# Three groups of narrow matmuls per batch instead of eight, in a kernel whose order is written out by hand

## The chip, the cores and the metric

The kernel runs on one core of one Trainium2 chip. The metric is the device time of one execution in microseconds (us), the median of several runs. PE is the matmul engine (PEld its weight loads), DVE the vector engine, ACT the activation engine, POOL the general-purpose engine, SP the engine whose queue issues all the DMAs here. PSUM is the memory that PE writes to; it has eight banks of 512 fp32 columns, and DVE and ACT empty it.

## The reference

Attention between 512 tokens and 32 state vectors in both directions, and then a two-layer network with a softplus between the layers, over all 8 x (512 + 32) rows.

```
# x: (8, 8, 512, 64), state: (8, 8, 32, 64); w_in: (512, 2048), w_out: (2048, 512)
scores = scale * np.matmul(x, state.transpose(0, 1, 3, 2))
a = softmax(scores)                      # over the 32 states
xread = np.matmul(a, state)
scores2 = scale * np.matmul(state, x.transpose(0, 1, 3, 2))
a2 = softmax(scores2)                    # over the 512 tokens
sread = np.matmul(a2, x)
rows = concatenate([xread, sread], axis=2)   # heads side by side: 512 columns
h = rows @ w_in
out = (log(1 + exp(h)) @ w_out).astype(np.float32)
```

## The kernel before

One batch has 512 token rows (and 32 state rows). The token rows never form `xread`: the kernel multiplies the state by `w_in` first (*state product*, `v_product`, letter v; it gives two PSUM banks for 512 of the 2048 columns), splits the result into a high and a low part (`v_hi` h, `v_lo` l), and multiplies those by the softmax weights (*gemm1*, letter g: six matmuls of 128x512 for 128 of the 2048 columns, into one PSUM bank). Softplus (s, ACT) reads that bank.

For batches 0 and 1 the second layer is *gemm2* (G) with `w_out` split in high and low parts. Batches 2 to 7, and the state rows of all batches (called batch 8), go another way: per batch seven sums of blocks (*forms*, F), each split (H high, L low) and multiplied by a combination of `w_out` blocks that lies in HBM as a *slab* (J loads it, 1 MB). A *product* (M) is half a form: eight pairs of matmuls, one of 512 columns with the high part and one of 256 with the low part. Fourteen products make a batch. `chain` (k) adds the results from PSUM, `fold` (q) adds halves, `fold_store` (P) stores.

The attention of one batch is four kinds of *narrow* PE work. *Scores* (Q, eight matmuls with tiles of 64 rows by 32 columns, two PSUM banks; they need the x loads T). The same tiles make the state product v, four units of eight matmuls per batch. Two *transposes* (t) of the column softmax; the *read* (R, 32 matmuls with 128x32 tiles); one transpose of the read's result (`s_back`, y). The softmax over states goes `a_turn` (1), `a_max` (2), `a_sub` (3), `a_exp` (4), `a_sum` (5), `a_mul` (6), `a_back` (7), `a_hi` (8), `a_lo` (9); the one over tokens `s_max` (e), `s_exp` (f), `s_sum` (i). The exponentials (4 and f) and softplus need different tables on ACT. In the profile an fp32 matmul leaves two records, so a v or a scores step shows as x16; gemm1 and the products show as what they are. gemm1 reads `b<-d,d`, gemm2 `b<-g,s`, products `b<-g,d`, v `b<-W,ST`, scores `b<-d,ST`, transposes `b<-ident`, the read `b<-d,s`.

Nothing schedules this kernel: the string `PLAN` has a letter for each step, and the last loop runs the steps in that order; every engine executes its share strictly in that order (class `Ordered`). Which of two engines does a step is looked up in `ENG` by the letter and its count (A is ACT, D is DVE, P is POOL; for the raw weights g and d name the pool). Buffers come from four pools with fixed numbers of rooms (`N1`, `N2`, `N4`, `N8`) and from the eight banks, first freed first taken, in the order of the plan. Every recorded operation has line 99, that of the class that records the order, so groups are told by their tiles.

```
    for k in PLAN:
        now[0] = k
        count[k] = count.get(k, 0) + 1
        next(run[k])
```

Of the kernel before, what the change touches and what calls it, by code (L numbers as in the profile page):

```python
# [37 lines left out]
PLAN = (
    "TSTISTTIIQII1IQ2Ie3OaXbfI1Ic4tO2vuOQ5hhOIla6IbI73aSc88O4e9vOa9Ohh5fatlla6ub7ac88b1919cgblcavbbgIehhlflcAgcAsbt"
    "XBcgIBICumvCDnDEsEhGmhslsGnmBAIenGOlBfgiCAmigDsCEGDsnaEgbO2OG2a3casGb3bOgacbGBcAcmRsCvnDGBAmTEhmGrAlhnGml4nAg4"  # L40
    "CnDgBTsEjBGCsCDBGjDmEAEgn5aGjsCt65GDujaGEbO6bOgaabOcAGjcsbGccjmBGOmBCAOnvDnjvAEhmChGhlhDAjlGllgEBjnAGsCBTgDCmE"
    "jgDBTnsEvsCQXihDXihGlmjleEGjefG1n17gXmf7XAjBGn88CsG9j9BGiAmignjDCtsEGDuEjG223g34jGgs5jt6sGu4QojvopNeGNphhefgjl"
    "olopUgpfm1yjtsWRzKYRZvKrs1njmuvhNGhmlhlhjGllnmgNjrUGsnGmWnKgYGNKsNnGmUgnWNvsNKYGhhlKGmlUmgnWGnsNKYGNKg5GUms6nG"
    "WmKgYnKGsNGNUmgnWGsKYGmKnNgGsGN7Ug8m79WGnsKG8YmJ9gKNNGsnJmUyGzZWngJYKGsKmGnJgitisGuGgGsGgGsyGz2Z32g34GsG5o6voH"
    "pogph7hplovlsp4LghghlslgFs5gsH6gs7LgsgFsgsHFgsLgsgsMsHFLMJFFHFMXLHJkXkSHMHJLHLFMJHkkqLPMHJqLPRJHkkvLMHrLhhllMJ"
    "HLMJkkLLyMJ8z89Z9MJkkqkPkqMPJvJkkMqhqhPlPlMTTJgJkkqvqsPgPhhlglsgsgsHvsLghhlglsgsgsHgsLgsgFsgsHgsLgsgFsFMsHFLQJ"
    "FMeHefLMXFJkXkF1f1HMHJHLHLMJHkkqLPMHJqLPiitFJtuMkuHkLLMJHLLRJHkkMr223L4yMJz3Z455vJk6Mhkhkqk6PllqMJ7P78899vJkkM"
    "qhqhPlPlMTTJgJkkqvqsPgPhlhglsgsgsHvsLghhlglsgsgsHgsLgsgFsgsHgsLgsgFsFMsHFLQJFMeHefLMXFJkXkF1f1HMHJHLHFLMJHMHkJ"
    "kqLPtqJktuPMkHuLLMJHiiLLRHJkMkrL22y3MJzL4Z354vJMk6hkhkqkqPlPMlJ5768vJkkMqh7hqPl8Pl9MT9TJgJkkqvqsPgPhlhglsgsgsH"
    "vsLghhlglsgsgsHgsLgsgFsgsHgsLgsgFsFMsHFLQJFMeHefLMXFJkXkF1f1HMHJHLHFLMJHMHkJkqLPtqJktuPMkHuLLMJHiiLLRHJkMkrL22"  # L50
    "y3MJzL4Z354vJMk6hkhkqkqPlPMlJ5768vJkkMqh7hqPl8Pl9MT9TJgJkkqvqsPgPhlhglsgsgsHvsLghhlglsgsgsHgsLgsgFsgsHgsLgsgFs"
    "FMsHFLQJFMeHefLMXFJkXkF1f1HMHJHFLHwMJHkxkMHJLLqtqJtwkPMukHPuLwLMJHxiiLLRHJwkMxrkL2xyMJ2zZ334L4vJkMkhqkhPkqlPwl"
    "Mx55v6Mh6hkkqlPlqM7P78899vkwgkqhxhPlqwgslwPxgxsgsJgswxvsghhlJglsgsgsJgsgsgsJgsgsgsgsgsgswwxxgswwxxgswwxxgswHHx"
    "LLgsHHLLgFFsHHLgFLsMFsHHLLFFMJFFFFHMJkkHkLLFFHMJFLHHLHHFLHMJHHkHHkFkLMJqFqPqPHLHMHPLJHkkkLLMJLHHLLLMHJHkkkLLLM"
    "JLLLMJkkqkPkqkkqMPPMkkqkPqqMPPMkqMPkqkqPP"
)
ENG = {
    '3': "PPPPPDPDPDPDPDDD",
    '6': "DDPPDPPDPPPPPPDD",
    '8': "AAAAAAAAAAAAAAAAAA",  # L60
    '9': "PPPPDDPDDDDDDDDDDD",
    'D': "AAPDDAAAAPPDAPAD",
    'E': "DDDDDDDDDDDDDPDD",
    'F': "DDDDDDPDDDDDDDPDDDDDDDPPDDDDDDPPDDDDDDPPPDPDDDDDDDDDPPPP",
    'H': "DAAAAAAAAAAAAAAAAAAADAAAAPAAAAAAAADAAAAPAAAAAAAADAAAAPAAAAAAAADAAAAPAADADDAAADAPAAAAAAAAPAAAPAAAAP",
    'I': "ggggggggggdgdddg",
    'L': "DDDDDDDDDDDDDDDDDDDDDDDDDDDDDDDDDDDDDDDDDDDDDDDDDDDDDDDDDDDDDDDDDDDDDDDDDDDDDDDDDDDDDDDDDDDDDDDDDD",
    'N': "DPDDDDDDDDDDDDDD",
    'O': "gggggddgggddddgg",
    'U': "DDDDDDDD",  # L70
    'W': "DDAAAAAA",
    'Y': "DDDDDDDD",
    'h': "AAAAAAADDAAAAAAAAAAAAAAAAADAAAAAADAAAAAADAAAAAAADAAAAAAADAAAAAAAAAAD",
    'k': "AADDDDDDDDDDDDDDAADDDDDDDDDDDDDDAADDDDDDDDDDDDDDAADDDDDDDDDDDDDDAADDDDDDDDDDDDDDADADDDDDDDDDDDDDDDDDDDDD",
    'm': "AAAAAPPADAAPAPPDPAPAAAAAAAAAAAAA",
    'n': "DDPDDDDDDDDDDPDDPDDDDDDDDDDDDDDD",
    'o': "DAAADAAA",
    'q': "PDPPPDPDPDPPPDPDPDPPPPPDPDPPPPPDDDPPPPPPDDDPPPPDDDDD",
    'u': "AAAADADAAAAAAAAA",
    'w': "AAAPAAAPPDDDDDDD",  # L80
    'x': "PPPPPDDDDDDDDDDD",
    'z': "DAAAAAAA",
}


# [898 lines left out]
```

## Time and profile before

| | |
|---|---|
| runs | 635.24 us median of 3 (634.68 to 636.11) |
| profiled execution | 634.05 us, its span 632.3 us |
| busy in the span | PE 613.6 us, DVE 486.6, ACT 326.8, POOL 123.0 |
| chain that ended last | PE 83% of the span, DVE 1%, ACT 1% |
| ACT_TABLE_LOAD | 36, of 1.28 us each |

The page's busy time of PE counts matmuls whose ends are modelled, and neighbours overlap in it. Prices of PE work are therefore read from starts: from the start of one line of the timeline to the start of the next. From about 200 us on the batches repeat with a period of some 69.5 us.

### The profile page before, as it was taken

What the parts mean: (1) busy time and instruction counts of PE and PEld (TensorE: products, weight loads), DVE (VectorE), ACT (ScalarE), POOL (GpSimd) and SP (SyncE); (2) the same over time, 40 slices, a digit from 0 to 9 for tenths busy, and PEclk for the clock granted to TensorE, in tenths of its full rate; (3) what the DMA queues carried; (4) which work ended last, traced back from release to release, by engine and by line L of the source; (5) the groups of instructions that cost most, each with busy time, mean ns of one, the idle gap of its engine ahead of it and who ended that gap; (6) DMA issues with size and microseconds to landing.
All of it is one profiled execution on the core that took longest, in us unless ns stands there. A gap on an engine that the chain in (4) does not pass through costs nothing.

```text
span 632.3 us, 10553 instructions
## 1 busy us (share of the span) xinstructions
PE 613.6 (97%) x4072; PEld 485.3 (77%) x4072; DVE 486.6 (77%) x741; ACT 326.8 (52%) x497; POOL 123.0 (19%) x108
## 2 busy tenths in 40 slices
PE   3799999999999999999999999999999999999997
PEld 1477777778878887888777877788778877998886
DVE  5999898999366964499638994599549994289993
ACT  4799969454375613662357434562367335332700
POOL 1121222100000200011202230042203522014440
PEclk9999999999999999999999999999999999999999
DMA  8999472645910998079923996099905947005672
GB/s 314 407 407 348 155 242 71 217 144 181 346 68 12 412 403 338 2 288 420 329 95 131 396 381 224 7 355 403 360 8 210 404 169 281 2 3 167 215 314 69
DMA packets 48049, 146.96 MB, mean 232 GB/s; under 512 B 4224, under 2 KB 28288, under 8 KB 37248
## 3 DMA queue, kind: packets, MB, share of 16 engines
q1 hardware_dynamic: 48000, 146.29, 61.8%
q8 instruction: 32, 0.52, 0.3%
q14 instruction: 17, 0.14, 0.1%
HBM read 122.68 MB, written 23.59 MB: 231 GB/s over the span
## 4 chain that ended last, share of the span: by engine, by line
PE 83%; DVE 1%; ACT 1%; issue 0%
PE b L99 83%; DVE s L99 1%; DVE d L99 1%; ACT L99 0%; ACT s L99 0%; DVE g L99 0%; ACT d L99 0%
## 5 line engine op out<-in xcount | busy, mean ns | idle before, releaser
L99 PE MATMUL b<-g,d 128*128 128x512 f32 x1344 | 252.1, 340 | 0.1
L99 PEld LDWEIGHTS b<-g,d 128*128 128x128 f32 x1344 | 205.7, 188 | 41.7 <-issue 10.9
L99 PE MATMUL b<-d,d 128*128 128x512 f32 x768 | 185.9, 394 | 1.9 <-ACT d L99 1.8
L99 PEld LDWEIGHTS b<-d,d 128*128 128x128 f32 x768 | 143.6, 189 | 43.3 <-issue 5.8
L99 DVE TENSOR_TENSOR d<-g,d 128x1024 fp32r<-128x1024 f32 x72 | 99.0, 1388 | 44.9 <-ACT d L99 44.5
L99 PE MATMUL b<-g,s 128*128 128x512 f32 x496 | 123.7, 382 | 0.8 <-DVE g L99 0.7
L99 PEld LDWEIGHTS b<-g,s 128*128 128x128 f32 x496 | 87.9, 188 | 25.4 <-issue 4.2
L99 ACT ACTIVATE g<-b 128x512 f32<-128x512 f32 x96 | 57.0, 597 | 77.9 <-PE b L99 77.8
L99 ACT CAST d<-g 128x1024 fp32r<-128x1024 f32 x59 | 61.2, 1050 | 33.7 <-PE b L99 16.3
L99 DVE TENSOR_TENSOR s<-s,b 128x512 f32<-128x512 f32 x91 | 57.4, 677 | 27.2 <-PE b L99 27.2
L99 POOL TENSOR_TENSOR g<-g,g 128x1024 f32<-128x1024 f32 x10 | 25.9, 2592 | 141.6 <-DVE g L99 81.8
L99 ACT CAST d<-b 128x512 fp32r<-128x512 f32 (+2 forms) x60 | 30.7, 561 | 33.4 <-PE b L99 33.3
L99 ACT ACT_TABLE_LOAD x35 | 44.9, 1283 | 2.3 <-DVE v L99 1.7
L99 POOL TENSOR_TENSOR s<-s,v 128x512 f32<-128x512 f32 x19 | 20.6, 1089 | 128.2 <-DVE v L99 111.4
L99 DVE TENSOR_TENSOR d<-b,d 128x512 fp32r<-128x512 f32 (+2 forms) x68 | 41.6, 650 | 3.5 <-ACT d L99 2.5
L99 POOL TENSOR_TENSOR s<-s 128x256 f32<-128x256 f32 x32 | 23.8, 752 | 101.2 <-DVE s L99 89.0
L99 PE MATMUL b<-W,ST 64*32 64x512 f32 (+2 forms) x544 | 36.3, 590 | 2.7 <-DVE W L99 2.7
L99 DVE TENSOR_TENSOR d<-d,d 128x1024 fp32r<-128x1024 f32 (+1 forms) x22 | 27.1, 1243 | 1.0 <-ACT d L99 0.9
L99 ACT ACTIVATE s<-b 128x512 f32<-128x512 f32 x32 | 18.6, 599 | 14.2 <-PE b L99 14.0
L99 ACT COPY s<-b 128x512 f32<-128x512 f32 x32 | 17.8, 589 | 14.8 <-PE b L99 14.6
L99 ACT CAST d<-d 128x1024 fp32r<-128x1024 f32 x18 | 18.8, 1048 | 10.6 <-DVE d L99 8.0
L99 DVE TENSOR_TENSOR s<-s,s 128x512 fp32r<-128x512 f32 x31 | 21.8, 709 | 2.4 <-ACT s L99 2.4
(77 smaller groups left out, 521.4 us busy)
## 6 DMA issues: line engine op xcount, KB each, us to landing
g<-slabs SPq DMA_DIRECT2D x84, 1024.0 KB, 8.9
d<-in_xt_dram SPq DMA_DIRECT2D x16, 512.0 KB, 6.2
d<-in_xn_dram SPq DMA_DIRECT2D x16, 512.0 KB, 7.2
slabs<-d SPq DMA_DIRECT2D x16, 512.0 KB, 3.2
g<-in_w_in_dram SPq DMA_DIRECT2D x12, 512.0 KB, 10.4
slabs<-g SPq DMA_DIRECT2D x24, 256.0 KB, 5.5
out_dram<-s SPq DMA_DIRECT2D x48, 128.0 KB, 4.3
g<-in_w_out_dram SPq DMA_DIRECT2D x10, 512.0 KB, 10.2
```

What stands on the lines that cost most here:

```text
L99: return lambda *a, **k: self.tc.keep_in_program_order(f(*a, **k))
```

## The change

Only the plan, the table of engines and two pool sizes change. From batch 2 on the narrow work of a batch stands in three groups: scores and two state products; the back transpose of the batch before and the two transposes; the read and two state products. Before it stood in eight: scores; two transposes; the read; the back transpose; four state products one by one. The order of all other steps is laid out anew around this, in the first 200 us and the last batch too, and many steps change between ACT, DVE and POOL. `N2` goes from 18 rooms to 20, `N4` from 14 to 13. No function is touched, and the matmuls are the same ones.

```
-N1, N2, N4, N8 = 4, 18, 14, 8
+N1, N2, N4, N8 = 4, 20, 13, 8
 PLAN = (
...
-    "vsLghhlglsgsgsHgsLgsgFsgsHgsLgsgFsFMsHFLQJFMeHefLMXFJkXkF1f1HMHJHLHFLMJHMHkJkqLPtqJktuPMkHuLLMJHiiLLRHJkMkrL22"
-    "y3MJzL4Z354vJMk6hkhkqkqPlPMlJ5768vJkkMqh7hqPl8Pl9MT9TJgJkkqvqsPgPhlhglsgsgsHvsLghhlglsgsgsHgsLgsgFsgsHgsLgsgFs"
...
+    "kkJqqPPMJgJkkqgqsPPgsQsvevefghhlhghlflgls1g1siHsgsiLgs2H23gs34gLgFs5gs6sg47HgLs5gsFMss6FHMXLJFFMXkJFkHFHMFLJHH"
+    "HytJztLuMukkqLPMJZqLPLMHJkkLH7RHJLvrvhhMHLllMJhhkllkMJHLMJ8k8kqkPkq9MPLTJ9MTkkJqqPPMJgJkkqgqsPPgsQsvevefghhlhg"
...
 )
 ENG = {
-    'h': "AAAAAAADDAAAAAAAAAAAAAAAAADAAAAAADAAAAAADAAAAAAADAAAAAAADAAAAAAAAAAD",
+    'h': "AAAAAAADAAAAAADADAADAAADAAAADAADDAAADADDDAAADADDDAAADADDDAAAAAAADAA",
...
```

Of the plan two lines of each side are shown; with the line that follows they hold one batch of the middle.

On PE, at the scores of a batch in the middle (the tiles that ST stands beside are the x of that batch for scores and `w_in` for the state product; `g` beside `d` is a product, `d` beside `d` gemm1). Before:

```order
L99 MATMUL b_194_3414<-g_56_3148,d_169_3289 128x512
L99 MATMUL b_194_3414<-g_56_3148,d_170_3303 128x256
L99 MATMUL b_195_3437<-d_165_3219,ST 32x512
L99 MATMUL b_196_3438<-d_165_3219,ST 32x512
...
L99 MATMUL b_195_3437<-d_166_3221,ST 32x512
L99 MATMUL b_196_3438<-d_166_3221,ST 32x512
...
L99 MATMUL b_193_3413<-g_57_3171,d_173_3342 128x512
```

The same place now:

```order
L99 MATMUL b_174_3243<-d_159_3139,d_151_3039 128x512 x3
L99 MATMUL b_175_3251<-d_161_3168,ST 32x512
L99 MATMUL b_176_3252<-d_161_3168,ST 32x512
...
L99 MATMUL b_175_3251<-d_162_3191,ST 32x512
L99 MATMUL b_176_3252<-d_162_3191,ST 32x512
...
L99 MATMUL b_177_3263<-W,ST 32x512
L99 MATMUL b_178_3264<-W,ST 32x512
...
L99 MATMUL b_179_3275<-W,ST 32x512
L99 MATMUL b_180_3276<-W,ST 32x512
...
L99 MATMUL b_181_3289<-d_158_3135,d_150_3037 128x512 x3
```

Scores stood alone between two products; now two state products stand right behind it, and all three between gemm1 steps.

On DVE, behind the same scores (the TENSOR_REDUCE are `s_max`; 128x1024 are forms). Before:

```order
L99 TENSOR_TENSOR d_180_3435<-g_63_3390,d_179_3432 128x1024
L99 TENSOR_TENSOR g_60_3248<-g_60_3248 128x4x256
L99 TENSOR_REDUCE v_11_3439<-b_195_3437 128x1
L99 TENSOR_SCALAR v_11_3439<-v_11_3439 128x1
L99 TENSOR_REDUCE v_11_3439<-b_196_3438 128x1
L99 TENSOR_SCALAR v_11_3439<-v_11_3439 128x1
L99 TENSOR_TENSOR d_182_3475<-g_60_3248,d_181_3469 128x1024
L99 TENSOR_TENSOR g_61_3301<-g_61_3301 128x4x256
```

Now (the rows with b_177 to b_180 are `v_hi` and `v_lo` of the two state products, of which DVE has two casts and four subtractions):

```order
L99 TENSOR_TENSOR s_230_2835<-s_230_2835,b_170_3173 128x512
L99 TENSOR_TENSOR s_231_2840<-s_231_2840,b_171_3174 128x512
L99 TENSOR_TENSOR s_231_2840<-s_231_2840 128x256
L99 TENSOR_REDUCE v_11_3253<-b_175_3251 128x1
L99 TENSOR_SCALAR v_11_3253<-v_11_3253 128x1
L99 TENSOR_REDUCE v_11_3253<-b_176_3252 128x1
L99 TENSOR_SCALAR v_11_3253<-v_11_3253 128x1
L99 CAST d_163_3296<-b_177_3263 128x512
L99 CAST d_164_3298<-b_178_3264 128x512
L99 TENSOR_TENSOR d_163_3296<-b_177_3263,d_163_3296 128x512
L99 TENSOR_TENSOR d_164_3298<-b_178_3264,d_164_3298 128x512
L99 TENSOR_TENSOR d_165_3301<-b_179_3275,d_165_3301 128x512
```

The maxima stood among the sums and splits of the forms; now two adds and a fold of the batch before stand ahead of them and the emptying of the state products' banks behind.

On ACT, among the softplus steps of a batch (`ACTIVATE g<-b` is softplus, `ACTIVATE s<-s` the row softmax's exponential). Before:

```order
L99 ACTIVATE g_61_3301<-b_182_3305 128x512
L99 ACTIVATE g_61_3301<-b_183_3317 128x512
L99 ACTIVATE g_61_3301<-b_184_3326 128x512
L99 CAST d_173_3342<-g_61_3301 128x1024
L99 ACTIVATE g_62_3351<-b_185_3334 128x512
L99 ACTIVATE g_62_3351<-b_186_3344 128x512
```

Now:

```order
L99 ACTIVATE g_64_3375<-b_186_3355 128x512
L99 ACT_TABLE_LOAD
L99 ACTIVATE s_243_3325<-s_243_3325 128x512
L99 ACT_TABLE_LOAD
L99 ACTIVATE g_64_3375<-b_187_3368 128x512
L99 ACTIVATE g_64_3375<-b_188_3379 128x512
L99 ACTIVATE g_64_3375<-b_189_3388 128x512
L99 ACT_TABLE_LOAD
L99 ACTIVATE s_244_3334<-s_244_3334 128x512
L99 ACT_TABLE_LOAD
L99 ACTIVATE g_65_3432<-b_190_3401 128x512
```

The two exponentials stood after all softplus steps of the batch, and stand now between them, each with a table load on both sides.

## Rows read from the trace of the kernel before

**Rows 1.** Page: busy time, and the granted PE clock in 40 slices.

```profile
PE 613.6 (97%) x4072; PEld 485.3 (77%) x4072; DVE 486.6 (77%) x741; ACT 326.8 (52%) x497; POOL 123.0 (19%) x108
PEclk9999999999999999999999999999999999999999
```

**Rows 2.** Timeline of PE in a batch: start, length, operation, count.

```profile
362.80 3.04 PE L99 MATMUL b<-g,d 128*128 128x512 f32 x16
365.68 0.27 PE L99 MATMUL b<-ident,v 128*128 128x128 f32 x1
365.71 3.02 PE L99 MATMUL b<-g,d 128*128 128x512 f32 x16
368.66 1.09 PE L99 MATMUL b<-W,ST 64*32 64x512 f32 x16
369.68 5.92 PE L99 MATMUL b<-g,d 128*128 128x512 f32 x32
375.53 1.09 PE L99 MATMUL b<-W,ST 64*32 64x512 f32 x16
...
384.80 5.75 PE L99 MATMUL b<-d,d 128*128 128x512 f32 x24
390.48 1.09 PE L99 MATMUL b<-W,ST 64*32 64x512 f32 x16
```

**Rows 3.** Timeline of PE where wide matmuls run without a break.

```profile
140.09 1.52 PE L99 MATMUL b<-d,d 128*128 128x512 f32 x6
141.45 2.88 PE L99 MATMUL b<-g,s 128*128 128x512 f32 x12
...
568.94 0.51 PE L99 MATMUL b<-g,s 128*128 128x512 f32 x2
569.29 0.87 PE L99 MATMUL b<-g,d 128*128 128x512 f32 x4
570.00 0.51 PE L99 MATMUL b<-g,s 128*128 128x512 f32 x2
```

**Rows 4.** Timeline of PE where a state product and scores stand together.

```profile
82.53 1.09 PE L99 MATMUL b<-W,ST 64*32 64x512 f32 x16
83.42 1.06 PE L99 MATMUL b<-d,ST 64*32 64x512 f32 x16
84.41 4.37 PE L99 MATMUL b<-g,s 128*128 128x512 f32 x18
```

**Rows 5.** Busy time by stretch: length, each engine, clock, DMA share, GB/s.

```profile
16.00:32.00 16.00, 12.62 (x81) 7.03 (x81) 15.35 (x36) 12.28 (x28) 2.75 (x4) 1.00 1.03 407
...
339.99:409.50 69.51, 69.51 (x474) 54.87 (x473) 52.46 (x72) 33.91 (x50) 14.29 (x12) 1.00 0.66 258
```

**Rows 6.** Timelines of PE and DVE behind scores: maxima, subtraction; v's subtractions and cast.

```profile
271.44 14.40 PE L99 MATMUL b<-g,d 128*128 128x512 f32 x80
271.76 0.68 DVE L99 TENSOR_REDUCE v<-b 128x1 f32<-128x512 f32 x1
...
273.34 2.20 DVE L99 TENSOR_TENSOR d<-g,d 128x1024 fp32r<-128x1024 f32 x1
...
302.12 1.28 DVE L99 TENSOR_TENSOR d<-b,d 128x512 fp32r<-128x512 f32 x2
...
315.44 0.69 DVE L99 CAST d<-b 128x512 fp32r<-128x512 f32 x1 [1.02 <-PE b L99]
```

**Rows 7.** Timeline of ACT: a table load, an exponential, a softplus.

```profile
272.95 1.28 ACT L99 ACT_TABLE_LOAD   x1
...
295.42 0.63 ACT L99 ACTIVATE s<-s 128x512 f32<-128x512 f32 x1 [2.18 <-POOL s L99]
...
318.35 0.60 ACT L99 ACTIVATE g<-b 128x512 f32<-128x512 f32 x1 [0.78 <-PE b L99]
```

**Rows 8.** Waits of PE's weight loads from 20 to 182 us: total, times, longest.

```profile
PEld b L99 <- DVE g L99: 2.5, 5, 0.7
```

**Rows 9.** Page: DMA issues, size each, median us to landing.

```profile
g<-slabs SPq DMA_DIRECT2D x84, 1024.0 KB, 8.9
d<-in_xt_dram SPq DMA_DIRECT2D x16, 512.0 KB, 6.2
```

More of the change, by code (lines that the diff above doesn't have):

```diff
@@ L38 @@
 PLAN = (
[L39 to L48, printed above, removed]
@@ L49 @@
-    "kqLPtqJktuPMkHuLLMJHiiLLRHJkMkrL22y3MJzL4Z354vJMk6hkhkqkqPlPMlJ5768vJkkMqh7hqPl8Pl9MT9TJgJkkqvqsPgPhlhglsgsgsH"
-    "vsLghhlglsgsgsHgsLgsgFsgsHgsLgsgFsFMsHFLQJFMeHefLMXFJkXkF1f1HMHJHLHFLMJHMHkJkqLPtqJktuPMkHuLLMJHiiLLRHJkMkrL22"
-    "y3MJzL4Z354vJMk6hkhkqkqPlPMlJ5768vJkkMqh7hqPl8Pl9MT9TJgJkkqvqsPgPhlhglsgsgsHvsLghhlglsgsgsHgsLgsgFsgsHgsLgsgFs"
-    "FMsHFLQJFMeHefLMXFJkXkF1f1HMHJHFLHwMJHkxkMHJLLqtqJtwkPMukHPuLwLMJHxiiLLRHJwkMxrkL2xyMJ2zZ334L4vJkMkhqkhPkqlPwl"
-    "Mx55v6Mh6hkkqlPlqM7P78899vkwgkqhxhPlqwgslwPxgxsgsJgswxvsghhlJglsgsgsJgsgsgsJgsgsgsgsgsgswwxxgswwxxgswwxxgswHHx"
@@ L54 @@
-    "LLgsHHLLgFFsHHLgFLsMFsHHLLFFMJFFFFHMJkkHkLLFFHMJFLHHLHHFLHMJHHkHHkFkLMJqFqPqPHLHMHPLJHkkkLLMJLHHLLLMHJHkkkLLLM"
-    "JLLLMJkkqkPkqkkqMPPMkkqkPqqMPPMkqMPkqkqPP"
+    "TSTSITIIIQII1IQ2Te3OaSbfX1Ic4I2vtOa5hOuOhla6IbI73aIc884lvba5hhallcae6bOfQ79Oc8I89evtbf19u19cAgOhbalhcgIlsbIbcg"
+    "cAmBvntCAghhDuBsECGlDslmGsEmBaengCGfnXBabIGmaDOAcsOgECGnDimsEGABBiG2aCRbDbcGmEbOnAgOAnOACGOsccGDarEgmBOnvCsBGB"
+    "C3hGhDlmalDtEgEAjAnugCs2DiGEsjBm34GCgnDb4bGEbbcaGamcAOGAnOcGcBBvCACDG5hhDlGsjEjEgTl6ATmg5sgni6sGmsjnjG7B8BTCmv"
@@ new lines @@
+    "9mCDvjhGjhlDjljGEEnQXnXG7AX181GAe9efGBfigCigTsGBCsDjmhthEgmlDultEsgnun2Gs2g334GsG5QXoo4vpmepGhf1nglhoe6optlfpy"
+    "R5zsRZ6r1vurvhhGlhlhlGmlngGjsjGmNjngGGmmnvGjGsNmUgnWngjsYKGjsKhjGNjljNGNUmgmWGnnsKgmngsjmGsGNNUGnWGNgGsYGmUKKg"
+    "YhlKGsnj7NGm7mnWgNNKUGsmYtWyGNzKZKUGJNWGNunjgNjNnGsUmJGngGsY88GYKmKnGKW9JUKGJYG9KWGooKYgpopo2pg2s3piKig34ygzs5"
+    "vZ6Ssvshgh7hl4lglhg5sl6gs7sgsgsgsgHHsLgsLHgsLgsgFsFMsFFMHJFFHFMJkkLLMHJHHFLMHJkHkqLPMXqLXPJLMJkkLvJvhhRHHlhMlH"
+    "hrllMJHkkLMJ8L9MJ8kkTqkPkq9MPLTJMJLkkqqMPPJgJkkqgqsPPgsQsvevefghhlhghlflgls1g1siHsgsiLgs2H23gs34gLgFs5gs6sg47H"
@@ new lines @@
+    "gLs5gsFMss6FHMXLJFFMXkJFkHFHMFLJHHHytJztLuMukkqLPMJZqLPLMHJkkLH7RHJLvrvhhMHLllMJhhkllkMJHLMJ8k8kqkPkq9MPLTJ9MT"
+    "kkJqqPPMJgJkkqgqsPPgsQsvevefghhlhghlflgls1g1siHsgsiLgs2H23gs34gLgFs5gs6sg47HgLs5gsFMss6FHMXLJFFMXkJFkHFHMFLJHH"
+    "HytJztLuMukkqLPMJZqLPLMHJkkLH7RHJLvrvhhMHLllMJhhkllkMJHLMJ8k8kqkPkq9MPLTJ9MTkkJqqPPMJgJkkqgqsPPgsQsvevefghhlhg"
+    "hlflgls1g1siHsgsiLgs2H23gs34gLgFs5gs6sg47HgLs5gsFMss6FHMXLJFFMXkJFkHFHMFLJHHHytJztLuMukkqLPMJZqLPLMHJkkLH7RHJL"
+    "vrvhhMHLllMJhhkllkMJHLMJ8k8kqkPkq9MPLTJ9MTkkJqqPPMJgJkkqgqsPPgsQsvevefghhlhghlflgls1g1siHsgsiLgs2H23gs34gLgFs5"
@@ L56 @@
+    "gs6sg47HgLs5gsFMss6FHMXLJFFMXkwJFkHwxFHMJHLHHxyLtJtzMuuwkxkLMJZqqPwLPMHxLJkRHwkJxLvvhhMlhlhllrLMJkkFM8J7wHHHx9"
+    "M8JLkkqMkPkqLPLMkkqw9PMxqwxPygkzkqZqgPsPwJgsxvsvhhglwhlJxhlgslgsgsJgsgsgsJgsgsgsgsgsgsgsgswwxxgswwxxgswwxxgsHH"
+    "HLHLgFFsLLgsHFHLgsLMFsHHLFFFMJLFFFHMJkkHkLLFFHMJFLHHLHHFLMJHHHHkFkkFLMJHHqqPqLHMLHHkPkPkJLLMHJHLLHHLMJkkkLLLMJ"
+    "LLLLMJkkqkPkqkkqMPPMkkqkPqqMPPMkqMPkqkqPP"
 )
 ENG = {
-    '3': "PPPPPDPDPDPDPDDD",
-    '6': "DDPPDPPDPPPPPPDD",
-    '8': "AAAAAAAAAAAAAAAAAA",
@@ L61 @@
[L61 to L66, printed above, removed]
+    '3': "PPDDDDPPPDPDPDPD",
+    '6': "DPPPPPPPDPDPDPDP",
+    '8': "AAAAAPAAAAAPAPAPAA",
+    '9': "PPPPPPDDDDDDDDDDDD",
+    'D': "PPDAADDPPAAPAPPP",
+    'E': "DDDDDDDDDDDDDDDD",
+    'F': "DDDDDDDDDDDDDDDPDDDDDDDPDDDDDDDPDDDDDDDDPDPDDDDDDDDDPPPP",
@@ L67 @@
+    'H': "ADAAAADAAPADPADAPAAAAAAAAAAADAPAAAAAAAAAAADAPAAAAAAAAAAADAPAAAAAAAAADADDAAADADAPAAAAAAAAPAAAAAAAAA",
+    'I': "ggggggggggggdddg",
     'L': "DDDDDDDDDDDDDDDDDDDDDDDDDDDDDDDDDDDDDDDDDDDDDDDDDDDDDDDDDDDDDDDDDDDDDDDDDDDDDDDDDDDDDDDDDDDDDDDDDD",
-    'N': "DPDDDDDDDDDDDDDD",
-    'O': "gggggddgggddddgg",
+    'N': "DDDDDDDDPDDDDDDD",
+    'O': "ggggggdgdggggdgg",
     'U': "DDDDDDDD",
-    'W': "DDAAAAAA",
+    'W': "AAAAAAAA",
     'Y': "DDDDDDDD",
-    'h': "AAAAAAADDAAAAAAAAAAAAAAAAADAAAAAADAAAAAADAAAAAAADAAAAAAADAAAAAAAAAAD",
+    'h': "AAAAAAADAAAAAADADAADAAAADAAAADAADDAAADADDDAAADADDDAAADADDDAAAAAAADAA",
@@ L74 @@
     'k': "AADDDDDDDDDDDDDDAADDDDDDDDDDDDDDAADDDDDDDDDDDDDDAADDDDDDDDDDDDDDAADDDDDDDDDDDDDDADADDDDDDDDDDDDDDDDDDDDD",
[L75 to L82, printed above, removed]
+    'm': "PPAPPADPPDDDAAAADAAADAAAAAAAAAAA",
+    'n': "DPDDDDDDDDDDDDDDPDDDDDDDDDDDDDDD",
@@ L83 @@
+    'o': "ADAAADAA",
+    'q': "PPPPPDPDPDPPPDPDPDPPPDPDPDPPPDPDDDPPPDPDDDDPPPPDDDDD",
+    'u': "AAAAAAAAAAAAAAAA",
+    'w': "PAAAPPAAAADDDDDD",
+    'x': "PPPPPPPPDPDDDDDD",
+    'z': "AAAAAAAA",
 }
```

## Prediction

> **What bounds the kernel now.** Three views, in this order. The page first: PE, the matmul engine, is busy for 97% of the span, and its clock is granted in full in every slice [rows 1]. So a change pays where it takes time off PE's own row of matmuls, or off PE's waits. Then busy time by stretch: from one scores step to the next (69.51 us, one batch) PE is busy for all of it, while DVE has 52.46 us of work and ACT 33.91 [rows 5]. In such a batch nobody is waited for, and only the order on PE can gain. Last, PE's timeline of that batch, for what the order itself costs. The reader is to compare starts: a stretch's price is the start of the next line minus its own.
>
> In an unbroken run the prices are these. Six gemm1 matmuls take 141.45 - 140.09 = 1.36 us, 0.2267 each [rows 3]. Three pairs of a product's matmuls (512 and 256 columns) take 570.00 - 568.94 = 1.06 us, 0.3533 a pair [rows 3]. Between two state products (v), 16 pairs take 375.53 - 369.68 = 5.85 us where 16 x 0.3533 = 5.65 would do, and 24 gemm1 matmuls take 390.48 - 384.80 = 5.68 where 5.44 would do [rows 2]. So a wide stretch that begins and ends at narrow matmuls pays 0.20 to 0.24 us more than its matmuls. After a transpose it pays 368.66 - 365.71 - 8 x 0.3533 = 0.12, and between a read and a transpose 365.68 - 362.80 - 2.83 = 0.05 [rows 2]. A v that stands alone takes 369.68 - 368.66 = 1.02 us [rows 2]. One with another narrow step right behind it takes 83.42 - 82.53 = 0.89, and that next one 84.41 - 83.42 = 0.99 [rows 4].
>
> **The change, part by part.** *Grouping.* No matmul is added or removed. I count both orders from the first gemm2 matmul on. The wide stretches go from 52 to 30. Between narrow and narrow (v or scores on both sides) they go from 21 to 7, from transpose to narrow from 8 to 4, from read to transpose from 4 to 0; the other kinds change by one or two in both directions and cancel. The same 36 narrow steps stand in 18 groups instead of 32, so 14 more of them have another right behind. Price: 14 x 0.22 (the mean of 0.20 and 0.24) = 3.1 us, 4 x 0.12 = 0.5, 4 x 0.08 = 0.3 (between the read's 0.05 and the transpose's 0.12), and 14 joins at 1.02 + 1.02 - 1.88 = 0.16 each for a pair and 0.15 in a group of three, so 14 x 0.15 = 2.1 us. Sum 6.0 us, all of it on PE, which no other engine hides. Bounds: if only the joins pay, 2.1; at 0.24 a stretch and 0.16 a join, 6.5.
>
> *What the groups ask of the others.* Scores and two v fill six PSUM banks in a row. The third gemm1 behind them takes the bank of the first v (its DVE wait stands in the new order). DVE must by then have made two maxima, two casts and one subtraction. From the end of scores that is 0.32 us until it starts (271.76 against PE's next stretch at 271.44), 1.58 for the maxima and what belongs to them (273.34 - 271.76), 2 x 0.69 and 0.64 [rows 6], together 3.9 us. PE needs 0.89 + 0.99 + 0.13 (half a surplus) + 2 x 1.36 = 4.7 us to get there. Slack 0.8 us, so I cost it at nothing. Its cover is those two gemm1 steps; without it, every microsecond that DVE is late costs up to 6 us, one per batch.
>
> *ACT's exponentials.* The row softmax's two stand now between softplus steps, so the table is changed twice around each; over the program the order has 50 loads for 36. One costs 1.28 us, an exponential 0.63, a softplus 0.60 [rows 7]. Each detour is 3.2 us, in which PE makes 2.3 gemm1 steps. In the 13 gemm1 steps behind the group (13 x 1.36 = 17.7 us) ACT has 13 x 0.60 + 2 x 3.2 + about 2 us of casts = 16.2 us. It keeps pace, and the last block is wanted only after three more products (3 x 8 x 0.3533 = 8.5 us). Cost nothing; bound above, 3.2 us a batch if a detour should hold PE outright.
>
> The Trainium skill speaks against this part: "ScalarE: Activation LUTs", section "Table sets: the hidden batching unit", says to batch activations by table set, and puts a switch at about 2.7 us. The row says 1.28 us, and the row decides; at 2.7 the 13 steps would hold some 6 us more on ACT, and part of the 8.5 us cover would be gone.
>
> *The transfers.* The second load of the next x stands in SP's row ahead of the batch's last product, and scores wants it after that product and three gemm1 (2.8 + 4.1 = 6.9 us). Its median to landing is 6.2 us [rows 9], and its buffer's last reader is the batch's fourth product from the end, so it can go sooner. Nothing. The product weights take 8.9 us in the median [rows 9]. A load stands two or three products ahead of its own in SP's row, two more often than before, behind output stores that wait for folds; it starts when a buffer comes free and has about three products (3 x 2.83 = 8.5 us) and the narrow groups between. That is tight on paper, yet the steady batch of before shows no wait of PE [rows 5]. Nothing, with up to 1 us a batch as the bound above.
>
> *The first 35 us.* By order the first gemm2 has 24 gemm1 matmuls and seven narrow steps ahead of it in both kernels, and DVE has 59 instructions to do for it instead of 57; the fifth wants 95 instead of 103. DVE does 36 in 15.35 us there [rows 5], 0.43 each: +0.9 us at the first, -3.4 at the fifth. PE's weight loads wait 2.5 us in all for DVE's gemm2 weights between 20 and 182 us [rows 8]. I take zero, with bounds of 2.5 us gained and 2 lost (the first w_in piece is now loaded behind the second state load, which moves the softmax's chain too).
>
> *Sum.* The profiled execution took 634.05 us: a span of 632.3 and 1.75 around it. 634.05 - 6.0 = 628.05. The median of the runs is 635.24, 1.19 above it, so the forecast is 635.24 - 6.0 = 629.2 us.
>
> **The rivals.** *DVE does not free the banks (slower).* The place is the third gemm1 behind scores, v, v. It decides from the work that DVE still has when scores ends: one 128x1024 subtraction of 2.20 us [rows 6] in its way makes it 2.20 - 0.8 = 1.4 us late, six batches 8.4 us, and 635.24 - 6.0 + 8.4 = 637.6. Against it: three gemm1 (4.1 us) lie between the last product and scores, and DVE has two adds and a fold to do in them. For it: such a subtraction is what stands around the maxima in the order of before. The skill has this as a rule too: "TensorEngine Tiling (Array Packing)", section "PSUM Bottleneck", warns that packed matmuls outrun the emptying of PSUM; no row of before shows such a wait.
>
> *The products wait (no change).* Softplus falls behind its detours, or weights land late, and the products wait about 1 us a batch: six batches give the 6.0 back, 635.2. ACT's 16.2 us against 17.7 speak against it; that the two are so close, and the weights' 8.9 against 8.5, for it.
>
> *The stretches' surplus does not follow the boundaries.* If it belongs to gemm1 and products as such, only the joins pay: 635.24 - 2.1 = 633.1. Against it: 0.12 after a transpose and 0.05 after a read, with the same matmuls.
>
> *The first 35 us get worse.* 3 us are lost there: 632.2.
>
> **How the numbers follow.** Forecast 0.70; surplus unmoved 0.08; worse start 0.08; products waiting 0.08; DVE late 0.06. Within 0.2% (1.3 us, about what a measurement of this kernel can tell from no change) falls the case of the waiting products: same 0.08. Slower 0.06. Faster 0.70 + 0.08 + 0.08 = 0.86. The range: below, 6.5 from the groups, 2.5 from the start and 0.7 of scatter, 635.24 - 9.7 = 625.5; above, to the case in which only the joins pay, 633.2. That leaves out the last two cases, 0.14.
>
> **What would show it.** From one scores step to the next PE should take 68.2 us instead of 69.51 (two joins in the first group and one behind the read give 0.45, five stretches fewer 0.9). A lone v should hardly be found after batch 2, and the stretch between v pairs should still pay about 0.2. Wrong would be: idle of PE at the third gemm1 behind a group, released by DVE; at a product, released by ACT; a first gemm2 later than 33 us. If the period is 69.5 or more, the grouping step is refuted; if it is 68.2 and the total has not fallen, the start is.

## The result, and the profile after

The changed kernel takes 628.67 us (median of five runs, 628.37 to 629.63) against 635.24 (now five runs, 634.45 to 636.11): a ratio of 0.9901, with a 95% interval of 0.9887 to 0.9916. The forecast was 629.2 in a range of 625.5 to 633.2. A second set of runs gave 628.85, a ratio of 0.9896 (0.9882 to 0.9910).

The page of the profiled execution (629.35 us, its span 627.5) has the same PE instructions, 5.8 us less busy time on PE than [rows 1], and on ACT 49 table loads where the page of before has 35 (the orders have 50 and 36, the number told ahead of the prediction):

```profile
PE 607.8 (97%) x4072; PEld 488.1 (78%) x4072; DVE 500.3 (80%) x759; ACT 328.7 (52%) x491; POOL 123.6 (20%) x110
...
L99 ACT ACT_TABLE_LOAD x49 | 62.9, 1283 | 6.5 <-DVE v L99 5.7
```

From one scores step to the next PE now takes 68.23 us. The view by stretch (length, PE, PEld, DVE, ACT, POOL, clock, DMA share, GB/s) answers the last of [rows 5]: PE is still busy all the time, and DVE and ACT have 4.0 and 2.3 us more to do in a shorter batch.

```profile
247.26:315.49 68.23, 68.23 (x474) 55.37 (x473) 56.44 (x77) 36.20 (x50) 11.50 (x10) 1.00 0.66 257
```

PE's timeline of one batch (start, length, operation, count) shows the three groups, where [rows 2] had narrow steps one by one:

```profile
315.49 1.09 PE L99 MATMUL b<-d,ST 64*32 64x512 f32 x16
316.38 1.92 PE L99 MATMUL b<-W,ST 64*32 64x512 f32 x32
318.23 17.98 PE L99 MATMUL b<-d,d 128*128 128x512 f32 x78
336.05 11.46 PE L99 MATMUL b<-g,d 128*128 128x512 f32 x64
347.34 0.27 PE L99 MATMUL b<-ident,v 128*128 128x128 f32 x1
347.45 1.04 PE L99 MATMUL b<-ident,s 128*128 128x128 f32 x8
348.24 8.57 PE L99 MATMUL b<-g,d 128*128 128x512 f32 x48
356.74 1.10 PE L99 MATMUL b<-d,s 128*32 128x64 f32 x64
357.77 1.95 PE L99 MATMUL b<-W,ST 64*32 64x512 f32 x32
359.65 20.06 PE L99 MATMUL b<-g,d 128*128 128x512 f32 x112
...
383.73 1.09 PE L99 MATMUL b<-d,ST 64*32 64x512 f32 x16
```

Scores and two state products take 318.23 - 315.49 = 2.74 us, where three lone steps would take 3.06.

Where the time went, by three landmarks on PE: the first gemm2, the first product and the end of the last matmul. Of the changed kernel:

```profile
33.45 0.39 PE L99 MATMUL b<-g,s 128*128 128x512 f32 x1
...
200.37 1.79 PE L99 MATMUL b<-g,d 128*128 128x512 f32 x9
...
620.38 2.99 PE L99 MATMUL b<-g,d 128*128 128x512 f32 x16
```

The same of the kernel before:

```profile
31.46 0.49 PE L99 MATMUL b<-g,s 128*128 128x512 f32 x1
...
200.51 1.79 PE L99 MATMUL b<-g,d 128*128 128x512 f32 x9
...
625.15 2.94 PE L99 MATMUL b<-g,d 128*128 128x512 f32 x16
```

| | before | changed | difference |
|---|---|---|---|
| first gemm2 starts | 31.46 | 33.45 | +1.99 |
| from there to the first product | 169.05 | 166.92 | -2.13 |
| from there to PE's end | 427.58 | 423.00 | -4.58 |

So from the first gemm2 on 6.7 us are gone, and 2.0 came back in the first 33 us of these two executions. Whether the 2.0 are the new order's is the second question below.

### The profile page after: what moved, and what is told of

Read it like the earlier page. It is cut to its first block, busy times and chain, and to the rows that moved or that the text cites. A ratio compares the mean times of both kernels' runs of the same rounds, so it can differ in the third digit from the quotient of the medians.

```text
span 627.5 us, 10514 instructions
## 1 busy us (share of the span) xinstructions
PE 607.8 (97%) x4072; PEld 488.1 (78%) x4072; DVE 500.3 (80%) x759; ACT 328.7 (52%) x491; POOL 123.6 (20%) x110
## 4 chain that ended last, share of the span: by engine, by line
PE 94%; DVE 3%; DMA 1%; ACT 0%; issue 0%; SPq 0%; ACTq 0%
PE b L99 94%; DVE s L99 1%; DMA g<-in_w_in_dram 1%; DVE v L99 1%; DVE W L99 1%; SPq L99 0%; ACT s L99 0%; DVE d L99 0%; ACT d L99 0%; DVE g L99 0%; ACTq L99 0%
## 5 line engine op out<-in xcount | busy, mean ns | idle before, releaser
L99 PE MATMUL b<-g,d 128*128 128x512 f32 x1344 | 249.0, 340 | 0.0
L99 PE MATMUL b<-d,d 128*128 128x512 f32 x768 | 182.6, 393 | 0.0
L99 PE MATMUL b<-g,s 128*128 128x512 f32 x496 | 121.7, 381 | 0.3 <-DVE g L99 0.3
L99 DVE TENSOR_TENSOR d<-g,d 128x1024 fp32r<-128x1024 f32 x72 | 101.3, 1416 | 9.3 <-POOL d L99 4.2
L99 ACT ACTIVATE g<-b 128x512 f32<-128x512 f32 x96 | 53.4, 600 | 73.7 <-PE b L99 49.1
L99 ACT CAST d<-g 128x1024 fp32r<-128x1024 f32 x55 | 56.5, 1052 | 28.6 <-PE b L99 18.2
L99 POOL TENSOR_TENSOR s<-s,v 128x512 f32<-128x512 f32 x19 | 23.4, 1233 | 123.0 <-issue 50.3
L99 ACT CAST d<-b 128x512 fp32r<-128x512 f32 (+2 forms) x47 | 24.4, 551 | 32.6 <-PE b L99 32.0
L99 DVE TENSOR_TENSOR d<-d,d 128x1024 fp32r<-128x1024 f32 (+1 forms) x22 | 27.6, 1258 | 6.8 <-PE b L99 5.1
L99 PEld LDWEIGHTS b<-W,ST 64*32 64x32 f32 x544 | 8.8, 108 | 24.4 <-issue 11.5
L99 DVE TENSOR_TENSOR g<-g,g 128x1024 f32<-128x1024 f32 x19 | 27.5, 1452 | 0.0
```

Source lines behind the costliest of these rows:

```text
L99: return lambda *a, **k: self.tc.keep_in_program_order(f(*a, **k))
```

## Experiments

Three questions: is it the boundaries of the groups that pay, and why; what does the new start cost; and how near are the waits that were costed at nothing. All runs are compared with runs of the kernel before on the same chip.

| run | median us | ratio to before (95%) |
|---|---|---|
| the changed kernel again | 628.85 | 0.9896 (0.9882 to 0.9910) |
| groups partly split again | 631.71 | 0.9949 (0.9935 to 0.9962) |
| kernel before with pairs alone | 632.6 | 0.9956 (0.9943 to 0.9968) |
| changed, first 33 us of before | 628.96 | 0.9901 (0.9887 to 0.9915) |
| changed, one load swapped | 629.01 | 0.9895 (0.9879 to 0.9911) |
| changed until 200 us, then before | 637.2 | 1.0025 (1.0015 to 1.0035) |
| the same with the pools of before | 634.91 | 0.9994 (0.9985 to 1.0003) |
| before until 200 us, then changed | 629.82 | 0.9912 (0.9899 to 0.9926) |
| DVE later behind scores | 634.57 | 0.9995 (0.9986 to 1.0004) |
| last batch's add first | 628.69 | 0.9903 (0.9886 to 0.9919) |
| before, state products of the whole array | 647.66 (one run) | no interval |
| the kernel before again | 634.96 (one run) | no interval |

### Part of the grouping undone

Parts of lines of the plan: behind the scores (changed so in four batches) and behind the read (in three).

```
...
-sQsvevefghhlhghlfl
+sQsveefgvhhlhghlfl
...
-LvrvhhMHLllM
+LvrhhMvHLllM
...
```

> The changed kernel with part of the grouping undone: in four batches the second state product behind the scores stands one gemm1 later, in three of them the second one behind the read stands one product later; nothing else moves. Seven joins are lost and seven wide stretches between narrow and narrow added. Theory (each boundary is paid for): 7 x (0.15 + 0.22) = 2.6 us, the median is 631.4, and PE takes 68.23 + 0.74 = 68.97 us from one scores step to the next. Rival (only the joins pay, the surplus belongs to the wide matmuls as such): 7 x 0.15 = 1.05, so 629.9, and 68.53. Rival (the gain is in the rest of the new order): 628.8 and 68.23.

Measured: 631.71, 2.9 above the changed kernel. PE's timeline from one scores step to the next:

```profile
316.69 1.09 PE L99 MATMUL b<-d,ST 64*32 64x512 f32 x16
317.57 1.06 PE L99 MATMUL b<-W,ST 64*32 64x512 f32 x16
318.57 1.65 PE L99 MATMUL b<-d,d 128*128 128x512 f32 x6
320.15 1.09 PE L99 MATMUL b<-W,ST 64*32 64x512 f32 x16
321.17 16.63 PE L99 MATMUL b<-d,d 128*128 128x512 f32 x72
...
385.66 1.09 PE L99 MATMUL b<-d,ST 64*32 64x512 f32 x16
```

The batch takes 385.66 - 316.69 = 68.97 us, to the hundredth what the boundaries predict. The six gemm1 matmuls that now stand alone take 320.15 - 318.57 = 1.58 for 1.36 of work, so 0.22 is their surplus, and the lone state product 1.02. The rivals (68.53, 68.23) are out: the matmuls are the same, and only where they stand has changed.

### The pairs alone, in the order of before

Parts of lines of the plan, for one batch; three batches are changed so.

```
...
-Z354vJMk6hkhkqkqPlPMlJ5768vJ
+Z354vvJMk6hkhkqkqPlPMlJ5768J
...
-kkqvqsPgPhlhglsgsgsHvs
+kkqvvqsPgPhlhglsgsgsHs
...
```

> The kernel before with one thing of the change alone: in batches 4 to 6 (three pieces of two) the second and the fourth lone state product stand right behind the first and the third; every other step, its casts too, stays where it was. Six joins more, six wide stretches between narrow and narrow less. Theory (the boundaries are the gain and need no new order): 6 x (0.15 + 0.22) = 2.2 us, so 635.2 - 2.2 = 633.0, and a batch takes 69.51 - 0.74 = 68.77 us. Rival (the banks that the joined products hold for 6 to 17 us longer make PE wait, which is why the rest was laid out anew): the stretches shrink alike, but PE waits for banks about as much, and the median is 635.2 or more.

Measured: 632.6, so 2.6 us gained with nothing else changed. PE's starts of two scores steps:

```profile
339.11 1.09 PE L99 MATMUL b<-d,ST 64*32 64x512 f32 x16
...
407.64 1.09 PE L99 MATMUL b<-d,ST 64*32 64x512 f32 x16
```

A batch takes 68.53 instead of the expected 68.77, and PE has no wait that the kernel before has not. Two joins gave 0.98 where 0.74 was reckoned: 0.56 for the pair with products between (both steps with the stretch between and the one behind took 15.12 us before and take 14.56), 0.41 for the pair with gemm1 between (25.73 and 25.32). The rival falls: the banks held for longer made nobody wait. These are two fifths of the gain of the change, without its new order.

### A state product without a change of the tile's shape

```
-            heads([a[:, 0:c1 - c0] for a in t], b, lambda q: W[:, q, c0:c1])
+            if b < 2:
+                heads([a[:, 0:c1 - c0] for a in t], b, lambda q: W[:, q, c0:c1])
+            else:
+                for e in range(2):
+                    nc.tensor.matmul(t[e][:, 0:c1 - c0], ident[:], W[:, e, c0:c1], start=True, stop=True)
```

From batch 2 on this kernel leaves the state out of these products.

> The kernel before, whose lone state products of batches 2 to 7 are made by two fp32 matmuls of the whole 128x128 array and 512 columns (the identity as weights, so that a part of the result is another one) instead of eight of 64x32 in quarters. Theory (the surplus is the change of the tile's shape on PE): the wide stretches beside them lose their surplus, 24 gemm1 between two of them take 5.44 to 5.50 us instead of 5.68, 16 pairs 5.65 to 5.70 instead of 5.85. Rival (the surplus follows any break in the row of wide matmuls, such as other weights or the fp32 kind): they stay at 5.68 and 5.85. The step itself may take 0.8 us (from four transposes of 128 columns, 0.40) or more; that decides nothing.

Read by its first row, the stretch of 24 gemm1 did not get shorter, as expected, but longer: 328.37 - 322.50 = 5.87. PE's timeline around it:

```profile
321.18 1.88 PE L99 MATMUL b<-W,ident 128*128 128x512 f32 x4
322.50 6.04 PE L99 MATMUL b<-d,d 128*128 128x512 f32 x24
328.37 1.88 PE L99 MATMUL b<-W,ident 128*128 128x512 f32 x4
```

The weight loads tell why. In this run, at the first row's step:

```profile
321.18 0.19 PEld L99 LDWEIGHTS b<-W,ident 128*128 128x128 f32 x1
321.61 0.19 PEld L99 LDWEIGHTS b<-W,ident 128*128 128x128 f32 x1 [0.24 <-DVE s L99]
322.04 0.19 PEld L99 LDWEIGHTS b<-W,ident 128*128 128x128 f32 x1 [0.24 <-issue]
322.47 0.19 PEld L99 LDWEIGHTS b<-d,d 128*128 128x128 f32 x1 [0.24 <-issue]
```

The four records of the step come 0.43 us apart, each load one matmul ahead of its use, and the load at 322.47 is already that of the first gemm1, whose stamp at 322.50 therefore lies 0.4 us before the last record of the step is through. What counts is the time from step to step: 328.37 - 321.18 = 7.19, less 4 x 0.43 and 24 x 0.2267, leaves 0.03 us. (With 16 pairs of a product between, the rows at 305.17 and 312.53 give 7.36 - 1.72 - 5.65, which leaves nothing.) PE's timeline of the kernel before, at the lone state product whose successor stands at 390.48 [rows 2]:

```profile
383.78 1.09 PE L99 MATMUL b<-W,ST 64*32 64x512 f32 x16
```

The step from one to the next takes 390.48 - 383.78 = 6.70; less 5.44 that is 1.26, where a step that stands between narrow ones takes 0.88 to 0.89. So 0.37 are paid for each lone 64x32 step, and 0.03 for the whole-array one, which is fp32 too and has other weights. The single run of this kernel took 647.66 us, as each such step is itself longer, 1.72 us. The weight loads of before show the price at the boundary itself:

```profile
390.48 0.18 PEld L99 LDWEIGHTS b<-W,ST 64*32 64x32 f32 x16 [0.35 <-issue]
391.50 0.53 PEld L99 LDWEIGHTS b<-d,d 128*128 128x128 f32 x3 [0.84 <-issue]
```

Both loads start together with the matmul that uses them, at 390.48 and 391.50, not ahead of it. That the kind of step is what matters is shown here (eight matmuls of 64x32 tiles against two of the whole array; tile and number change together). That PE empties itself at the change is an explanation that fits. The Trainium skill states it: "TensorEngine Tiling (Array Packing)", section "Key Properties", says that a change of the tiling mode drains TensorE. The trace agrees, as no load runs ahead of its matmul there, and adds the price of 0.37 us a step.

### The start

The first two plans written as slices of the two plans, the third as its first letters:

```
 PLAN = changed
...
-PLAN = changed
+PLAN = before[:104] + changed[102:]    (less one b and one l)
...
-TSTSITIII
+TSTISTIII
```

These are the changed kernel again, the splice at 33 us, and the swapped load; a second profile of the kernel before stands beside them.

> The changed kernel once more, for a second profile and as the yardstick of the three runs beside it. The profiled execution of it ended 4.7 us before that of the kernel before, while the medians lie 6.57 us apart. If the 2.0 us that the first gemm2 came later (33.44 against 31.46) are its order's, the first gemm2 starts at 33.4 within 0.3 again and the median is 628.7 within 0.7. If they are scatter of the first transfers, the first gemm2 moves by over 0.5 from execution to execution.

> The changed kernel with the first 104 steps of the plan of before (up to about 33 us), their engines too; the rest is the changed one. If the start of the changed order costs 2.0 us, the first gemm2 is back at 31.5, nothing else moves, and the median falls by 2.0, to 626.7. If the later start is given back behind it (by DVE or the transfers, which are busy until 60 us), or was scatter, the median stays at 628.7 within 0.7.

> The changed kernel with one letter moved: the first w_in piece is loaded ahead of the second state load, as before. Theory: part of the 2.0 us is this load, whose landing DVE waits for at 9.54 (8.90 before); it lands 0.6 earlier, the first state product starts at about 12.0 instead of 12.56, and the median falls by 0.6, to 628.1. Rival: the chain that ends last there is the other one (scores, the two softmaxes, whose second half waits for the second x load at 7.36), and nothing falls: 628.7.

> The kernel before once more, for a second profile. Its first profile ended 1.2 us under the median. Theory (the first profile caught early first transfers): the second scores step starts at 7.6 within 0.3 instead of 6.82, the first gemm2 at 32.4 within 0.5 instead of 31.46, the time is 635.3 within 0.6, and from the first gemm2 to the last matmul PE takes 596.6 as before. Rival (the start is as it was, other stretches vary): the first gemm2 at 31.5, and 596.6 grows to 597.5 or more.

The changed kernel's first gemm2 came at 33.36 the second time, that of the kernel before at 32.69 instead of 31.46. PE's timeline of that second profile of before, at the second scores step, 12 gemm1 and the landmarks:

```profile
7.71 1.11 PE L99 MATMUL b<-d,ST 64*32 64x256 f32 x16 [1.55 <-DMA d<-in_xt_dram]
...
26.09 3.83 PE L99 MATMUL b<-d,d 128*128 128x512 f32 x12
29.76 0.60 PE L99 MATMUL b<-ident,s 128*128 128x128 f32 x4
...
32.69 1.57 PE L99 MATMUL b<-g,s 128*128 128x512 f32 x5
...
201.23 1.09 PE L99 MATMUL b<-g,d 128*128 128x512 f32 x5
```

In the first profile of before that scores step started 0.89 earlier (first row); in that of the changed kernel it lay between (second row):

```profile
6.82 1.11 PE L99 MATMUL b<-d,ST 64*32 64x256 f32 x16 [0.74 <-DMA d<-in_xt_dram]
...
7.36 1.11 PE L99 MATMUL b<-d,ST 64*32 64x256 f32 x16 [1.28 <-DMA d<-in_xt_dram]
```

So the second load of x lands up to 0.9 us earlier or later from execution to execution, and the start moves with it. Of the 1.23 us by which the second profile of before is later, 0.72 had come by the 12 gemm1 (26.09 instead of 25.37). The other 0.5 came at these matmuls, which took 29.76 - 26.09 = 3.67 us instead of 28.48 - 25.37 = 3.11. Busy time by stretch shows the clock granted to PE there (the last number but two), 0.50, the lower of its two levels:

```profile
17.60:27.60 10.00, 6.92 (x30) 3.81 (x31) 9.61 (x25) 6.25 (x19) 1.87 (x3) 0.50 1.03 409
```

From 9 to 16 us, ahead of it, PE was busy for 3.3 of the 7 us. In the first profile it was busy for 3.5 of them, and the clock stayed at 1.00.

What the order costs is read from the second scores step on. From there to the first gemm2 the kernel before takes 31.46 - 6.82 = 24.64 us, and 24.5 to 24.8 in the three other profiles with its start and the full clock. The changed kernel takes 33.45 - 7.36 = 26.09, the second time 26.27, and 25.6 to 27.1 in the five other profiles with its start. So of the 1.99 us 0.54 are the load's scatter and 1.45 the order's. But they cost nothing further on. By the first product the changed kernel is level: 200.37, 200.26 and 200.53 (swapped load) against 200.51 and 201.23; over all runs it is 200.24 to 201.33 with the start of the changed plan and 200.51 to 201.23 with that of before. The splice with the start of before reached its first gemm2 at 33.12 and its first product at 200.75 only, and its median is the same, 628.96. The swapped load gained nothing either (629.01). The theory that 2.0 us were to be had there falls.

### Before and behind 200 us

```
-PLAN = changed
+PLAN = changed[:714] + before[713:]    (less one S)
...
+N2, N4 = 18, 14    (second run)
...
+PLAN = before[:713] + "S" + changed[714:]    (third run)
```

> The first 714 steps of the changed plan (up to the first product, 200 us), and from there on the plan of before with its eight narrow groups a batch, its engines too, in the changed pools. Theory (the narrow groups make the gain): PE takes 427.6 us from the first product to its last matmul as before, instead of 423.0, so the median is 628.7 + 4.6 = 633.3, and from one scores step to the next PE takes 69.5. Rival (the new order of the first 200 us or the two pools make it): the median stays within 1 us of 628.7.

The first of these was 3.9 us slower than expected. Its batches take 69.5 us, as expected (scores at 340.48 and 410.00), and its end has a wait that neither kernel has. PE's timeline there:

```profile
593.59 0.74 PE L99 MATMUL b<-g,d 128*128 128x256 f32 x3 [2.24 <-DVE d L99]
```

> The run with the changed first 714 steps and the rest of before, once more, with the pools of before (18 and 14 rooms instead of 20 and 13). That run was 3.9 us slower than expected, and its trace has one wait of PE that neither kernel has: 2.24 us for DVE at 593.6. Theory (a room of the smaller pool N4 comes free late there): the wait is gone and the median falls by 2.2 to 635.0. Rival (the wait is of the spliced order): 637.2 and the same wait.

With the pools of before the wait is gone and the median is 634.91. The order of before wants its own pools (which of the two it is, `N4` with a room fewer or `N2` with two more, is not shown). The 1.6 us that are left above the 633.3 first expected are the gain that this sum granted to the first 200 us: they alone give 635.23 - 634.91 = 0.3 us, inside the interval of no change.

> The first 713 steps of the plan of before (to the first product, 200 us), and from there on the changed plan with its engines and pools. Theory: PE takes 423.0 us from the first product to its last matmul, as in the changed kernel, instead of 427.6; the gain of the first 200 us is missing: 635.2 - 4.6 = 630.6. Rival (the first 200 us add nothing, all of the 6.4 is behind them): 628.8.

The counterpart, 629.82, has 5.4 of the gain; its first product starts at 201.02, and PE ends at 622.94, 421.9 later. So the gain lies behind 200 us, in the batches with three groups, and what the first 200 us add is 0.3 to 1.0 us.

### How near the bank is

```
-                nc.vector.tensor_reduce(nm(b, e), sc[b, e, 0].t, AX.X, ALU.max)
+                for _ in range(4 if b >= 4 and e == 0 else 1):
+                    nc.vector.tensor_reduce(nm(b, e), sc[b, e, 0].t, AX.X, ALU.max)
```

The expectation rests on these rows of DVE in the changed kernel, behind the scores at 315.49:

```profile
316.67 0.69 DVE L99 TENSOR_REDUCE v<-b 128x1 f32<-128x512 f32 x1 [3.73 <-PE b L99]
...
319.45 2.48 DVE L99 TENSOR_TENSOR d<-b,d 128x512 fp32r<-128x512 f32 x4
```

> The changed kernel with the first maximum of batches 4 to 7 taken four times instead of once, which puts 3 x 0.69 = 2.06 us more on DVE right behind the scores, ahead of the casts and subtractions that free the first state product's bank. In the profile of the changed kernel the first of these subtractions ends at 320.07, and the third gemm1 behind the group would start at 318.22 + 0.11 + 2 x 1.36 = 321.05, so DVE has 0.98 to spare. Theory (the bank decides at the third gemm1): PE waits there 2.06 - 0.98 = 1.1 us in each of four batches, released by DVE, and the median is 628.8 + 4.3 = 633.1. Rival (more room than it seems, or the wait is given back within the batch): 628.8 within 0.7.

Measured: 634.57, 5.7 above the changed kernel. PE's timeline and its waits (total, times, longest):

```profile
316.92 1.09 PE L99 MATMUL b<-d,ST 64*32 64x512 f32 x16
...
319.65 3.02 PE L99 MATMUL b<-d,d 128*128 128x512 f32 x12
323.88 1.40 PE L99 MATMUL b<-d,d 128*128 128x512 f32 x5 [1.20 <-DVE d L99]
...
386.62 1.09 PE L99 MATMUL b<-d,ST 64*32 64x512 f32 x16
```

```profile
PE b L99 <- DVE d L99: 4.8, 4, 1.2
```

PE waits at the third gemm1, in each of four batches, as the theory has it. But the price was mis-sized: a batch takes 386.62 - 316.92 = 69.70 us, 1.47 above 68.23, and 4 x 1.47 = 5.9 is what was lost. The subtractions start 4.95 us behind the first maximum (323.05 against 318.10) instead of 2.78, so DVE was 2.17 later. The third gemm1 would have started at 319.65 + 0.11 + 2 x 1.36 = 322.48 and starts at 323.88, 1.40 later (the wait in the row, 1.20, is counted from the modelled end of the matmul ahead). So the slack was 2.17 - 1.40 = 0.77, not 0.98: between the end of the subtraction that frees the bank and the matmul that takes it some 0.2 us more pass.

### The one wait that the change added

In the last batch of the changed kernel the pair of state products behind the read is longer than elsewhere:

```profile
494.24 2.46 PE L99 MATMUL b<-W,ST 64*32 64x512 f32 x32
496.63 3.68 PE L99 MATMUL b<-g,d 128*128 128x512 f32 x19
```

DVE, whose adds free the banks, is at a subtraction of 128x1024 from 492.65 on, for 2.31 us, and the add starts at 494.88. The edit, in a part of a line of the plan:

```
...
-MHxLJkRHwkJxLvv
+MHxJkLRHwkJxLvv
...
```

> The changed kernel with one letter moved in the last batch: an add of DVE that frees a bank stands ahead of a 128x1024 subtraction instead of behind it. In the profile of the changed kernel the two state products behind the read of the last batch take 2.39 us (494.24 to 496.63) where the other batches take 1.88, since DVE is at that subtraction for 2.31 us and the add starts at 494.88 only. Theory: the pair takes 1.88 and PE's last matmul ends 0.5 earlier; the median falls by 0.3 to 0.5, to 628.4, about what the runs scatter. Rival (the subtraction was awaited too, by the product behind): the wait moves to that product, and nothing falls.

Measured: the pair takes 1.87 (PE's rows at 494.25 and 496.12), so the wait is gone as the theory says.

From the first product to PE's end it took 422.62 us instead of 423.00, so 0.38 of the 0.5 arrived at the end. The median, 628.69, is 0.2 under that of the changed kernel in its own second set and that of its first: a gain of this size is in the trace and can't be told by the runs.

## Why the prediction was right

**What bounds the kernel.** PE is full before and after, at the full clock from 40 us on. The list of PE's waits in the changed kernel is empty from there on; the one late place that the change added, the pair of the last batch, shows by its length alone.

**Grouping, 6.0 us.** The counts hold: on PE's timeline the wide stretches go from 52 to 30. But all of this lies behind the first product, 37 stretches before and 15 now; between the first gemm2 and the first product there are 15 in both. So the term must be set against what was gained behind the first product, 4.6 us in the two profiles, and not against the 6.7 from the first gemm2 on. Two things that have nothing to do with the groups hold the 4.6 down. One is the 0.5 us of the last batch. The other is in the last 60 us, where PE has the same kinds of matmuls in the same order in both kernels: some fifty rounds of three pairs (512 and 256 columns). PE's timeline of the changed kernel has such a round every 1.06 us:

```profile
597.77 0.51 PE L99 MATMUL b<-g,s 128*128 128x512 f32 x2
...
598.83 0.51 PE L99 MATMUL b<-g,s 128*128 128x512 f32 x2
```

The run that has the changed plan from 200 us on has one every 1.04 us:

```profile
597.81 0.51 PE L99 MATMUL b<-g,s 128*128 128x512 f32 x2
...
598.85 0.51 PE L99 MATMUL b<-g,s 128*128 128x512 f32 x2
```

The first twenty rounds take 1.06 us each in every profile. The last thirty or so take 1.04 in both profiles of before and 1.06 in both of the changed kernel, so that this end takes 59.80 us (623.37 - 563.57) instead of 59.15 (628.09 - 568.94). What sets the pace no run shows; both values occur with the changed plan. In the run shown second PE takes 421.9 us from the first product to its end, 5.7 less than before. So the term was right in its mechanism and came out at 4.6 to 5.7 us.

By batch, 68.23 us were measured where 68.2 was forecast, and the stretch between a pair of state products and the next scores still pays about 0.2, as forecast: 383.73 - 359.65 - 56 x 0.3533 - 18 x 0.2267 = 0.21. The price of a join and a stretch, 0.15 + 0.22 = 0.37 us, came out as 0.37 in the split run and 0.49 with the pairs alone: its rows were those of stretches with gemm1, and a pair with products between gave 0.56.

**The third gemm1.** The slack, 0.8 by the forecast, was 0.77 by the delayed run, and nobody used it up: no such wait stands in the changed kernel. That the two agree so closely is luck: DVE was 0.2 us faster than reckoned (3.7 us from the end of scores, not 3.9), and the 0.2 us between the subtraction and the matmul were left out. The mechanism and the place of the rival were right, and so was its price for a group (1.4; the run lost 1.47), but there are four such groups in the plan and not six, so a subtraction of 2.20 us there would have cost some 6 us, not 8.4. The rule of the Trainium skill that was named there ("TensorEngine Tiling (Array Packing)", section "PSUM Bottleneck") thus holds here from a lateness of DVE of about 0.8 us on.

**Exponentials and table loads.** The profile has 14 table loads more, as counted. A detour took 3.24 us on ACT (its softplus steps end and start again at 327.56 and 330.80), as reckoned from [rows 7]. PE waits for ACT nowhere in the steady batches, and ACT is busy for 36.20 of 68.23 us. To cost them at nothing was right. The rule of the Trainium skill that was named there ("ScalarE: Activation LUTs", section "Table sets: the hidden batching unit"), to batch activations by table set, did not bite, as ACT has the room.

**Transfers.** From 40 us on PE waits for no slab and no x; the median slab landed in 7.7 us after its issue, against 8.9 in [rows 9].

**The first 35 us.** Here the step was weakest. The forecast took zero in bounds of 2.5 gained to 2.0 lost and named a first gemm2 later than 33 us as a sign of being wrong. That sign came (33.45, 33.36), and the total fell all the same. Three things were not seen. The new order itself is some 1.5 us later at the first gemm2, where 0.9 was reckoned. The second x in the profile of before landed earlier than in any of the other thirteen profiles, so the landmark of 33 us was set too early. And the first gemm2 decides nothing, as both kernels are level at the first product, at 200 us. The 2.1 us that the changed kernel gains between the two landmarks have no fewer stretches to come from. PE's weight loads wait there 0.7 us for DVE's gemm2 weights (20 to 182 us) where [rows 8] has 2.5; that fits the term for the fifth gemm2, but no run tests it.

**The sum.** 629.2 against 628.67. The closeness is in part luck: the groups gave 0.3 to 1.4 us less than their 6.0, and the first 200 us, for which the forecast had nothing, gave 0.3 to 1.0. The two profiles of each kernel account for 4.7 to 5.8 us of the 6.6 between the medians: the profiled executions of before (634.05 and 634.96) lie under its medians, those of the changed kernel (629.35 and 629.12) over its own. The slower pace at the end, 0.7 us, is in both profiles of the changed kernel; whether its other executions have it too no trace shows, so the rest stays open.
